# Two blocks of linear attention on one Trainium2 core: sums of x and of wq for the joint pair of q groups made in the k half and in o2 and kept, instead of being made in the joint stage

## The chip, the cores and the metric

One Trainium2 chip, one core. The time is the device time of one execution in microseconds, median of several runs. TensorE (PE) multiplies, with its weight loads shown apart (PEld); VectorE (DVE) and ScalarE (ACT) work element by element on 128 partitions; GpSimd (POOL) here does almost nothing but issue DMAs, as does SyncE (SP). DMAs move data between DRAM and the on-chip memory (SBUF); TensorE writes to PSUM.

## The reference

Two independent blocks, A and B, each with x of 2048 x 640, wqkv of 640 x 1920 and wo of 640 x 640, all fp32; 32 heads of width 20. For each block:

```python
qkv = (x @ wqkv)            # split into q, k, v, 32 heads of 20
phi = lambda t: jnp.where(t > 0, t + 1, jnp.exp(t)) + 1e-6
pq, pk = phi(q), phi(k)
kv = einsum("bhsd,bhse->bhde", pk, v)
z  = einsum("bhsd->bhd", pk)
num = einsum("bhqd,bhde->bhqe", pq, kv)
den = einsum("bhqd,bhd->bhq", pq, z)[..., None] + 1e-6
out = (num / den) @ wo      # heads put together
```

The two outputs stand side by side in one array of 2048 x 1280.

## The kernel before, in words

Every fp32 product is three products of rounded parts: a high part (`hi`, a ScalarE copy that rounds to the type fp32r) and a low part (`lo`, what is left, a VectorE subtraction in `low`, line 164). `mm3` (lines 174 to 176) adds hi x hi, lo x hi and hi x lo in PSUM.

x is handled in tiles of 128 rows, two tiles are a pair (p = 0 to 15), four tiles a group (0 to 3 of block A, 4 to 7 of block B).

**The k half.** For each pair k = x wk is made by a scheme with seven products in place of eight (`product`, `combine`): x is cut into quarter blocks A11 to A22 and a rest A5, and besides the raw parts it uses the sums S1 to S4 of them (`x_sum`, line 455). `x_parts` splits each of these into hi and lo; S1 and S3 lie in tiles `ksh`/`ksl`, which take turns between two buffers. Then comes phi (`ek`), its parts `pkh`, `pkl`, and G = x^T phi(k) gathered in `gacc` through PSUM `psg`. From G come KV, then M = KV wo, which is stored to DRAM (`md`, POOL, line 866), read back to `wst` (line 209), summed for the seven-product scheme, split into `fsh` and `fsl` (lines 902 and 164) and stored in DRAM (`fdmh`, `fdml`, POOL, line 911). Of the raw parts, the low ones are stored in DRAM too (`store_xt`, tile `xd`, SP, lines 247 to 260), and phi(k) goes out as `zd` (POOL, line 569). The order is one of jobs with a number for their place (`job`, `SHIFT`, `MOVED`), sorted by `perform`.

**The q half.** The line of stages is q0, q1, o0, q2, o1, q3, o2, q4, o3, q5, o4, r, o5, o6, o7. A q stage multiplies one group of x by wq, adds phi and builds the denominators (`acc` spread over DRAM as `da`, inverted, gathered as `rd`, line 1022); the division (line 1029), its split (`dah`, `dal`) and the sums of divided parts (`sr`, split into `dsh`, `dsl`) follow. An o stage multiplies by the forms of M and writes output rows (POOL, lines 1338 and 1340). Work beside TensorE is hung on slots of these stages with `at(slot, f)`, moved by an offset in the table `AT`.

**The joint stage r** (`qpair`, 46 slots of three 128x512 matmuls) makes q of the last two groups, 6 and 7, together, with the seven-product scheme over pairs of groups. Slots 0 and 1 use part 21; 2 to 7 part 11; 8 to 11 the sum S1 with the weight sum T; 12 to 15 S2 with `w23`; 16 to 21 part 12; 22 to 24 part 15; 25 to 31 S3 and 25; 32 to 39 part 22 with the weight sums Z and D, and 25; 40 to 45 S4. Its operands are made on the way there:

- wq of block B is loaded a second time (`load_w("w", ...)`), its sums are made in o3 and o4 (`wsum1`, `wsum2`, `wlast`), split and stored to DRAM (`wsmall`, tiles `wdT`, `wdZ`, `wdD`, line 1124), and read over the parts of wq no longer needed (`wback`, line 1140);
- the raw blocks of x are loaded (`load_xs`, line 1157), S1 to S4 are made from them in place by VectorE (`xs_sum`, line 1163), and split by ScalarE (`xs_split`, line 1179) and VectorE (line 164). The low parts of 11, 12 and 22 come from `xd` (line 1182), those of x5, the fifth chunk, from `xd` as well (line 1193), into a buffer that is shared with `sr`;
- `keep7` and `copy` (line 345) move PSUM `pa` to SBUF, so that the next product can use the bank.

Loads issue on SP in program order, and a queue's instruction waits for the buffer that it writes.

Of the kernel before, what the change touches and what calls it, by code (L numbers as in the profile page):

```python
# [15 lines left out]
DH = 20  # L16
# [90 lines left out]
def tile_linear_attn_pair(ctx: ExitStack, tc: tile.TileContext, ins, out: bass.AP):  # L107
# [22 lines left out]
    NGR = len(GROUPS)  # L130

# [106 lines left out]
    def store_xt(p, i):  # L238
        u, q = divmod(p, 2)
        lo = f32(ka[p, min(i, 1)][1])  # L240
        if u >= NU - 2:
            j = p - 2 * (NU - 2)
            if NU - 2 not in xd:
                xd[NU - 2] = dram.tile([P, NC, 2, 4, P], F32, name=f"xd{NU - 2}")
            d = xd[NU - 2][:, :, int(i == 1), j]
            if i == 0:
                nc.sync.dma_start(d[:, 0:4], lo)
# [13 lines left out]

    def load_xraw(u, c):
        b, g = divmod(u, NG)
# [193 lines left out]
    def pair_jobs(p, spots):  # L457
# [6 lines left out]
        x_parts(p, "S1", a + 1, [("s2", p)])  # L464
# [6 lines left out]
        x_parts(p, "S3", a + 1, [("s3", p)])  # L471
# [320 lines left out]

    def kv_hi(b, g):
        r = DH * GROUPS[g][1]
        t = kvt[b, g]
        kvt[b, g] = [base.tile([r, r], F32R, name=f"kv{x}", tag=f"kv{x}", bufs=6) for x in "hl"] + [t]
        nc.scalar.activation(kvt[b, g][0], t, AF.Copy)
# [283 lines left out]
    def wslots(k):  # L1081

        if k == 0:
            for c in (0, 2, 4):
                wst["w", 1, c] = stage("wst")
            wraw["x", 0], wraw["z", 0] = stage("wx"), stage("wz")
            for c in (1, 3):
                wst["w", 1, c] = stage("wst")
        else:
            wraw["x", 1], wraw["z", 1] = stage("wx"), stage("wz")  # L1090
            for a in ("11", "21", "22"):
                for c in range(2):
                    xw[a, c] = stage("xs")[:, :512]

    def wsum1(k):
        m, n = wst["w", 1, k], wst["w", 1, 2 + k]
        x = wraw["x", k]
        tt = nc.vector.tensor_tensor
        tt(x[:, HQ:2 * HQ], n[:, HQ:2 * HQ], m[:, HQ:2 * HQ], op=OP.subtract)
        tt(m[:, HQ:2 * HQ], m[:, HQ:2 * HQ], m[:, :HQ], op=OP.subtract)  # L1100

    def wsum2(k):
        m, n = wst.pop(("w", 1, k)), wst.pop(("w", 1, 2 + k))
        x, z = wraw["x", k], wraw.pop(("z", k))
        tt = nc.vector.tensor_tensor
        tt(x[:, :HQ], n[:, HQ:2 * HQ], m[:, HQ:2 * HQ], op=OP.subtract)
        tt(z[:, :HQ], n[:, :HQ], x[:, :HQ], op=OP.subtract)
        wraw["T", k] = m[:, :2 * HQ], 1
        wraw["Z", k] = z[:, :2 * HQ], 0

    def wlast(k):
        m = wst.pop(("w", 1, 4))
        nc.vector.tensor_tensor(m[:, HQ:2 * HQ], m[:, :HQ], m[:, HQ:2 * HQ], op=OP.subtract)
        wraw["D", k] = m[:, :2 * HQ], 1

    def wsmall_lo(kind, k):
        t, at = wraw[kind, k]
        h = [t[:, i * HQ:(i + 1) * HQ] for i in range(2)]
        nc.vector.tensor_tensor(h[at].bitcast(F32R), h[at], h[1 - at], op=OP.subtract)

    def wsmall_store(kind, k):
        t, at = wraw.pop((kind, k))
        d = dram.tile([P, 2 * HQ], F32, name=f"wd{kind}{k}")
        nc.gpsimd.dma_start(d, t)
        wsm[kind, k] = d, at

    def wsmall(kind, k):

        t, at = wraw[kind, k]
        h = [t[:, i * HQ:(i + 1) * HQ] for i in range(2)]  # L1130
        nc.scalar.activation(h[1 - at].bitcast(F32R), h[at], AF.Copy)
        later(1, wsmall_lo, kind, k)
        later(2, wsmall_store, kind, k)

    def wback(kind, k):
        d, at = wsm.pop((kind, k))
        i, c = {"T": (k, HQ), "Z": (0, k * HQ), "D": (1, 0)}[kind]
        for j, t in enumerate(whl["q", 1, i]):
            src = (1 - at, at)[j]
            nc.sync.dma_start(f32(t)[:, c:c + HQ], d[:, src * HQ:(src + 1) * HQ])  # L1140

    def w23_split(k):
        x = wraw.pop(("x", k))
        w23[k] = [base.tile([P, D], F32R, name=f"wf{t}", tag=f"wo{t}", bufs=2)[:, :2 * HQ] for t in "hl"]
        split(*w23[k], x[:, :2 * HQ])

    def xspan(b, c, t):
        return ins[b]["xt"][c * P:(c + 1) * P, (NG - 2) * 512:].rearrange("p (j t s) -> p t j s", t=2, s=P)[:, t]
# [10 lines left out]
    def xs_sum(n, c):  # L1159
        a11, a21, a22 = (xw.get((a, c)) for a in ("11", "21", "22"))  # L1160
        o, x, y, op = {1: (a22, a21, a22, OP.add), 2: (a22, a22, a11, OP.subtract),
                       3: (a21, a11, a21, OP.subtract), 4: (a22, xw.get(("12", c)), a22, OP.subtract)}[n]
        nc.vector.tensor_tensor(o, x, y, op=op)

    RAW = {"S1": "22", "S2": "22", "S4": "22", "S3": "21", "22": "22b"}

# [5 lines left out]
    def xs_split(a, c):  # L1172

        if a == "11":
            for k in range(2):
                xform("21", k)
        hi, lo = xform(a, c)
        src = xw[RAW.get(a, a), c]
        nc.scalar.activation(hi, src, AF.Copy)
        if a in ("11", "12", "22"):  # L1180
            k, t = chunk_of(a, c)
            nc.sync.dma_start(f32(lo).rearrange("p (j s) -> p j s", s=P), xd[NU - 2][:, k, t])
        else:
            later(1, low, lo, src, hi)
# [5 lines left out]
    def split_x5(t):  # L1190
        r = x5[t] = q2[0].tile([P, 2, 512], F32R, name="x5", tag="sr", bufs=2)
        nc.scalar.activation(r[:, 0], xw["5", t], AF.Copy)
# [115 lines left out]
    def outmm(u):  # L1308
# [14 lines left out]
        for s, (n, q) in enumerate(order):  # L1323
# [5 lines left out]
            where = [4 * g + 2 * q + t if u < NU - 2 else 4 * (NG - 2) + 2 * (2 * q + t) + (u == NU - 2) for t in range(2)]  # L1329
# [571 lines left out]
```

## Time and profile before

| | |
|---|---|
| median of 3 runs | 570.87 us (570.82 to 572.21) |
| the profiled execution | 571.82 us, of which the span of its instructions is 570.0 |
| TensorE busy | 561.5 us (98%) |
| VectorE, ScalarE, GpSimd busy | 441.1, 338.8, 87.2 us |
| moved by DMA | 131.53 MB, mean 231 GB/s |
| joint stage r | 481.04 to 515.86 us |

Rows of the timeline give the start, the length and the engine, then line, operation and tiles, and in brackets how long the engine stood idle before it and what released it. A group's row has the count after x, then busy time and mean ns. `x<-xd` means that tile x is written from tile xd. Times of DMA rows on SP and POOL are those of the issue; the landing is given separately.

### The profile page before, as it was taken

The page shows a single profiled execution, that of the slowest core. Times are in us where ns is not written, and L with a number is a line of the kernel's source. Part 1 is how long each engine was busy: PE and PEld are TensorE (multiplying, and loading weights), DVE is VectorE, ACT ScalarE, POOL GpSimd, SP SyncE. Part 2 cuts the span into 40 slices and gives each one's busy share as a digit, 9 for nine tenths or more (in the row PEclk, how much of TensorE's full clock was granted, in tenths as well). Part 3 has the DMA queues.
Part 4 walks back from the last instruction along what each step waited for, and adds up shares of the span by engine and source line. Part 5 has one row for each costly group of instructions (what it writes and reads, how often), then busy time and mean ns, then how long its engine had stood idle before and what let it go on. Part 6 is the DMA issues. An engine that isn't in the chain of part 4 may idle for free.

```text
span 570.0 us, 9167 instructions
## 1 busy us (share of the span) xinstructions
PE 561.5 (98%) x3219; PEld 508.7 (89%) x3219; DVE 441.1 (77%) x755; ACT 338.8 (59%) x635; POOL 87.2 (15%) x146
## 2 busy tenths in 40 slices
PE   9999999999999999999999999999999999999997
PEld 7989999898989988988888898898989888779997
DVE  6888798886684878878845987959668688979881
ACT  6874667672676874755737754737537274684441
POOL 0111133320011211232201103120012201000110
PEclk9999999999999999999999999999999999999999
DMA  8869789999895877989997977754568998820322
GB/s 282 234 154 260 179 243 309 268 333 353 294 246 123 202 197 156 357 207 270 356 317 228 347 229 240 248 164 159 175 214 280 308 390 248 264 81 0 131 93 92
DMA packets 85270, 131.53 MB, mean 231 GB/s; under 512 B 10088, under 2 KB 47592, under 8 KB 85224
## 3 DMA queue, kind: packets, MB, share of 16 engines
q1 hardware_dynamic: 72376, 89.75, 49.1%
q0 software_dynamic: 12560, 40.97, 26.0%
q8 instruction: 25, 0.41, 0.3%
q10 hardware_dynamic: 288, 0.23, 0.1%
q14 instruction: 21, 0.17, 0.1%
HBM read 77.09 MB, written 50.68 MB: 224 GB/s over the span
## 4 chain that ended last, share of the span: by engine, by line
PE 68%; DVE 12%; DMA 8%; issue 5%; ACT 3%; SPq 2%; POOL 0%; DVEq 0%; POOLq 0%; ACTq 0%
PE pa L341 15%; PE pe L341 7%; PE psg L176 7%; PE psg L175 7%; PE psg L174 7%; PE psk L602 5%; PE psb L341 5%; PE psq L174 4%; PE psq L176 4%; PE psq L175 4%; DMA wst<-in_B_wq 2%; PE pskv L784 2%; DMA xs<-in_B_xt 2%; DMA da<-acc 1%; DVE dsl L164 1%
## 5 line engine op out<-in xcount | busy, mean ns | idle before, releaser
L176 PE MATMUL psg<-pkh,xnl 128*128 128x512 f32 x160 | 62.8, 392 | 0.2 <-DVE xnl L164 0.2
L175 PE MATMUL psg<-pkl,xnh 128*128 128x512 f32 x160 | 62.8, 393 | 0.0
L174 PE MATMUL psg<-pkh,xnh 128*128 128x512 f32 x160 | 62.8, 392 | 0.0
L174 PE MATMUL psq<-xqh,wqh 128*128 128x512 f32 x150 | 59.1, 394 | 0.0
L176 PE MATMUL psq<-xqh,wql 128*128 128x512 f32 x150 | 58.5, 390 | 0.0
L175 PE MATMUL psq<-xql,wqh 128*128 128x512 f32 x150 | 58.4, 389 | 0.0
L345 ACT ACTIVATE o<-pa 128x320 f32<-128x320 f32 x64 | 27.6, 437 | 49.7 <-PE pa L341 49.6
L569 POOL DMA_DIRECT2D zd<-ek x30 | 26.2, 874 | 132.8 <-DVE ek L561 54.0
L345 ACT ACTIVATE ko<-pa 128x320 f32<-128x320 f32 x52 | 22.4, 432 | 36.7 <-PE pa L341 36.5
L176 PEld LDWEIGHTS psg<-pkh,xnl 128*128 128x128 f32 x160 | 30.0, 188 | 7.1 <-DVE xnl L164 0.8
L175 PEld LDWEIGHTS psg<-pkl,xnh 128*128 128x128 f32 x160 | 30.0, 188 | 5.8 <-DVE pkl L577 0.5
L174 PEld LDWEIGHTS psg<-pkh,xnh 128*128 128x128 f32 x160 | 30.1, 188 | 5.2
L176 PEld LDWEIGHTS psq<-xqh,wql 128*128 128x128 f32 x150 | 28.2, 188 | 6.0
L174 PEld LDWEIGHTS psq<-xqh,wqh 128*128 128x128 f32 x150 | 28.2, 188 | 5.7 <-ACT xqh L279 0.3
L175 PEld LDWEIGHTS psq<-xql,wqh 128*128 128x128 f32 x150 | 28.2, 188 | 5.4
L647 DVE TENSOR_TENSOR gacc<-psg,gacc 128x512 f32<-128x512 f32 (+2 forms) x42 | 25.6, 628 | 8.9 <-PE psg L176 8.9
L573 ACT ACTIVATE pkh<-ek,epst 128x640 fp32r<-128x640 f32 x32 | 25.9, 824 | 11.0 <-DVE ek L561 10.9
L1029 DVE SCALAR_TENSOR_TENSOR pq<-pq,rd 128x1280 f32<-128x1280 f32 x16 | 23.2, 1482 | 10.7 <-DMA rd<-da 10.7
L437 ACT ACTIVATE ksh<-sx 128x512 fp32r<-128x512 f32 x26 | 16.2, 629 | 25.2 <-DVE sx L455 25.0
L561 DVE SCALAR_TENSOR_TENSOR ek<-ek,ko 128x640 f32<-128x640 f32 x32 | 26.2, 820 | 6.0 <-ACT ko L558 3.4
L577 DVE SCALAR_TENSOR_TENSOR pkl<-ek,pkh 128x640 fp32r<-128x640 f32 x32 | 25.9, 820 | 5.7 <-ACT pkh L573 5.7
L967 DVE SCALAR_TENSOR_TENSOR pq<-pq,rq 128x512 f32<-128x512 f32 x30 | 20.6, 687 | 8.5 <-ACT rq L966 8.5
(290 smaller groups left out, 1781.9 us busy)
## 6 DMA issues: line engine op xcount, KB each, us to landing
zd<-ek POOLq DMA_DIRECT2D x32, 320.0 KB, 5.2
out<-o POOLq DMA_DIRECT2D x28, 320.0 KB, 4.2
xql<-xd SPq DMA_DIRECT2D x24, 256.0 KB, 4.6
xt<-in_B_xt_tiles SPq DMA_DIRECT2D x16, 320.0 KB, 4.4
xn<-in_B_x SPq DMA_DIRECT2D x16, 320.0 KB, 4.7
xqs<-in_A_xt SPq DMA_DIRECT2D x20, 256.0 KB, 6.4
fdmh<-fsh POOLq DMA_DIRECT2D x14, 320.0 KB, 4.4
fdml<-fsl POOLq DMA_DIRECT2D x14, 320.0 KB, 4.9
```

What stands on the lines that cost most here:

```text
L174: nc.tensor.matmul(o, whi, xhi, start=first, stop=False)
L175: nc.tensor.matmul(o, whi, xlo, start=False, stop=False)
L176: nc.tensor.matmul(o, wlo, xhi, start=False, stop=last)
L341: nc.tensor.matmul(o, x, y, start=start and m == r == 0, stop=m == len(terms) - 1 and r == 2, skip_group_check=True)
L345: nc.scalar.activation(x, y, AF.Copy)
L561: nc.vector.scalar_tensor_tensor(ek[n], ek[n], 1.0, rk[n], op0=OP.min, op1=OP.add)
L569: nc.gpsimd.dma_start(zacc[b], e, accum_op=OP.add)
L573: nc.scalar.activation(pk[n][0], ek[n], AF.Identity, bias=epst)
L577: nc.vector.scalar_tensor_tensor(lo, ek[n], EPS, f32(hi), op0=OP.add, op1=OP.subtract)
L602: nc.tensor.matmul(kps["c", n][h], plain_x(n, c)[i], plain_w(c)[j][:, h * HF:(h + 1) * HF], start=(c == 0 and i == j == 0), stop=(c == NC ...
L647: nc.vector.tensor_tensor(o, x, o, op=OP.add)
L1029: nc.vector.scalar_tensor_tensor(p, p, EPS, r, op0=OP.add, op1=OP.mult)
```

## The change

- **Groups are joined in another order.** `TG` maps the q groups' places: groups 5 and 6 (pairs 10 to 13) are the joint pair, and group 7 is done alone as the sixth q stage.
- **Kept forms of x.** In the k half, hi and lo of S1 and S3 of pairs 10 to 13 are stored to DRAM by POOL (`store_s`, 16 stores of 256 KB, tiles `sd`); with pairs as quarter blocks the S1 and S2 (S3 and S4) of the joint stage are two halves of what is stored. The joint stage reads them (`load_s`, 16 loads of 256 KB, on POOL and SP) and makes no sums and no splits of sums.
- **Sums of wq at its first load.** `wsum1`, `wsum2` and `wlast` run in o2 on the chunks that the first load brought. T, Z and D stay in SBUF in a tile `kept`, which takes the place of the split KV (`kvs`, now one tile); only the sum for `w23` goes to DRAM and back (two stores, two loads). The second load of wq, five stores and ten loads of 128 KB go. `wback` becomes a split of the kept sum by ScalarE and VectorE.
- **Low parts placed apart.** `xs_lo` and `x5_lo` load the low parts of 11, 12, 22 and x5 at slots of their own, not with the splits of the high parts.
- phi, mix and sums of the joint stage's halves are hung up to four slots earlier, and `AT` has other offsets.

```diff
+    TG = list(range(NG)) + [NG, NU - 1, NG + 1, NU - 2]
+    J0 = 2 * TG[NU - 2]
...
+    def store_s(p, i, k):
+        if (i, k) not in sd:
+            sd[i, k] = dram.tile([P, 2, 2, 4, P], F32, name=f"sd{i}{k}")
+        nc.gpsimd.dma_start(sd[i, k][:, :, :, p - J0], f32(ks[p, i][k]))
...
+    def s_stores(p, i, spot, what):
+        if J0 <= p < J0 + 4:
+            for k in range(2):
+                job(("ss", p, i, k), spot + k, store_s, p, i, k, after=[("xl", p, what)])
...
     def wsum1(k):
-        m, n = wst["w", 1, k], wst["w", 1, 2 + k]
-        x = wraw["x", k]
+        m, n = wst["q", 1, k], wst["q", 1, 2 + k]
+        x = wraw["x", k] = f32(base.tile([P, D], F32R, name="wx", tag="woh", bufs=2))
         tt = nc.vector.tensor_tensor
         tt(x[:, HQ:2 * HQ], n[:, HQ:2 * HQ], m[:, HQ:2 * HQ], op=OP.subtract)
-        tt(m[:, HQ:2 * HQ], m[:, HQ:2 * HQ], m[:, :HQ], op=OP.subtract)
+        tt(kept("T", k), m[:, HQ:2 * HQ], m[:, :HQ], op=OP.subtract)
...
     def wback(kind, k):
-        d, at = wsm.pop((kind, k))
         i, c = {"T": (k, HQ), "Z": (0, k * HQ), "D": (1, 0)}[kind]
-        for j, t in enumerate(whl["q", 1, i]):
-            src = (1 - at, at)[j]
-            nc.sync.dma_start(f32(t)[:, c:c + HQ], d[:, src * HQ:(src + 1) * HQ])
+        hi, lo = (t[:, c:c + HQ] for t in whl["q", 1, i])
+        split(hi, lo, kept(kind, k))
...
-    def xs_sum(n, c):
-        a11, a21, a22 = (xw.get((a, c)) for a in ("11", "21", "22"))
...
-        nc.vector.tensor_tensor(o, x, y, op=op)
...
+    def load_s(n, c):
+        i, f = divmod(n - 1, 2) if n < 3 else (1, n - 3)
+        for k, t in enumerate(xform(f"S{n}", c)):
+            (nc.sync if n == 2 or n > 2 and k else nc.gpsimd).dma_start(f32(t).rearrange("p (j s) -> p j s", s=P), sd[i, k][:, f, c])
...
+    for k in range(2):
+        i = 1 + 4 * k
+        at(("o", h - 1, i), wsum1, k)
+        at(("o", h - 1, i), wsum2, k)
+        at(("o", h - 1, i + 1), wx_store, k)
+        at(("o", O - 1, 9 + k), wx_load, k)
+        at(spot(4 + 4 * k), w23_split, k)
+    at(("o", h - 1, 11), wlast)
...
+        at(("o", O, 5 + c), load_s, 1, c)
+        at(("r", 2), load_s, 2, c)
+        at(("o", O, 7 + 3 * c), wback, "T", c)
+        at(("r", 6 + 2 * c), xs_lo, "12", c)
+        at(("r", 13 + c), load_s, 3, c)
+        at(("r", 2 + c), load_x5, c)
+        at(("r", 24 + c), load_s, 4, c)
```

TensorE's order stays, but for one product of the denominators that comes a product later. On POOL, at the end of the k half's stretch in which pairs 10 to 13 are made, there stood (line, tile written and read, shape; `md` is M, `fdmh` and `fdml` the forms of M):

```order
L866 DMA md_2178<-mev 20x4x640
L569 DMA zd_1927<-ek 128x640
L911 DMA fdmh_2854<-fsh 128x640
L911 DMA fdmh_2903<-fsh 128x640
L911 DMA fdml_2905<-fsl 128x640
```

and now:

```order
L256 DMA sd_2182<-ksl 512x1x128
L570 DMA zd_1927<-ek 128x640 x3
L873 DMA md_2171<-mev 20x4x640
L256 DMA sd_2068<-ksh 512x1x128
L256 DMA sd_2091<-ksl 512x1x128
L570 DMA zd_1927<-ek 128x640
L256 DMA sd_2172<-ksh 512x1x128
L918 DMA fdmh_2862<-fsh 128x640
L256 DMA sd_2182<-ksl 512x1x128
L918 DMA fdmh_2912<-fsh 128x640
```

Four stores of S of pair 13 came between the last M and the first forms; the other twelve stand earlier.

On VectorE, from the last reciprocal of the joint pair's predecessor to the split of its divided parts, there stood (`xs` the sums of x, line 1163; `o` output rows):

```order
L1016 RECIPROCAL da<-da 128x128
L1163 TENSOR_TENSOR xs<-xs 128x512
L348 TENSOR_TENSOR o_3690<-pe,o_3690 128x320
L1163 TENSOR_TENSOR xs<-xs 128x512 x2
L164 TENSOR_TENSOR xql<-xs,xqh 128x512
L348 TENSOR_TENSOR o_3690<-pe,o_3690 128x320
L164 TENSOR_TENSOR xql<-xs,xqh 128x512
L1163 TENSOR_TENSOR xs<-xs 128x512
L348 TENSOR_TENSOR o_3690<-pe,o_3690 128x320
L164 TENSOR_TENSOR xql<-xs,xqh 128x512
L1029 SCALAR_TENSOR_TENSOR pq<-pq,rd 128x5x256 x2
L1163 TENSOR_TENSOR xs<-xs 128x512 x2
```

and now (`kept` holds the sums of wq):

```order
L1023 RECIPROCAL da<-da 128x128
L344 TENSOR_TENSOR o_3692<-pe,o_3692 128x320
L152 TENSOR_TENSOR wql<-kept,wqh 128x256
L344 TENSOR_TENSOR o_3692<-pe,o_3692 128x320 x2
L1036 SCALAR_TENSOR_TENSOR pq<-pq,rd 128x5x256 x2
L1055 TENSOR_TENSOR sr<-pq 128x512
L1056 TENSOR_TENSOR sr<-sr,pq 128x512
L152 TENSOR_TENSOR dal<-pq,dah 128x1024
```

Between the reciprocal and the division (`pq<-pq,rd`) the sums and low parts of x are gone, and one low part of `kept` has come.

On SP, from the gather of the reciprocals into the joint stage, there stood:

```order
L1022 DMA rd<-da 32x4x128 x4
L1140 DMA wqh<-wdT_5332 128x256
L1140 DMA wql<-wdT_5332 128x256
L1140 DMA wqh<-wdT_5559 128x256
L1140 DMA wql<-wdT_5559 128x256
L1157 DMA xs<-in_B_xt 128x4x128 x2
L1188 DMA x_5763<-in_B_xt 128x4x128
```

and now:

```order
L1029 DMA rd<-da 32x4x128 x4
L1139 DMA xs<-in_B_xt 128x4x128
L1165 DMA xqh<-sd_2068 128x512
L1165 DMA xql<-sd_2091 128x512
L1169 DMA x_5691<-in_B_xt 128x4x128
L1165 DMA xqh<-sd_2068 128x512
L1165 DMA xql<-sd_2091 128x512
L1169 DMA x_5703<-in_B_xt 128x4x128
```

Four loads of S2 (256 KB each) stand where four loads of T's parts (128 KB each) stood, and x5's raw parts have come between them.

More of the change, by code (lines that the diff above doesn't have):

```diff
@@ L795, in kv_hi @@
         t = kvt[b, g]
-        kvt[b, g] = [base.tile([r, r], F32R, name=f"kv{x}", tag=f"kv{x}", bufs=6) for x in "hl"] + [t]
+        if b not in kvs_:
+            kvs_[b] = base.tile([P, 2 * NGR, 6 * DH], F32R, name="kvs", tag="kvs", bufs=1)
+        kvt[b, g] = [kvs_[b][:r, 2 * g + k, :r] for k in range(2)] + [t]
         nc.scalar.activation(kvt[b, g][0], t, AF.Copy)
@@ L1079, in tile_linear_attn_pair, with kept @@
     xw, xf, x5 = {}, {}, {}
[L1081 to L1093, printed above, removed]
+    def kept(kind, k):
+        if "kept" not in wsm:
+            wsm["kept"] = base.tile([P, 12 * 6 * DH], F32, name="kept", tag="kvs", bufs=1)
+        c = {"T": 0, "Z": 2, "D": 4}[kind] + k
+        return wsm["kept"][:, c * HQ:(c + 1) * HQ]
@@ L1116, in wsmall_lo @@
[L1116 to L1133, printed above, removed]
+        tt(x[:, :HQ], n[:, HQ:2 * HQ], kept("T", k), op=OP.subtract)
```

132 lines of the change are left out of this document (54 added, 78 removed).

## The prediction

> **What bounds the kernel now.** I read the page first, then the span cut into stretches, then the waits of TensorE, and last the rows around each stall of the stage that the change rewrites. In the page, busy time, share and instructions of each engine:
>
> ```profile
> span 570.0 us, 9167 instructions
> PE 561.5 (98%) x3219; PEld 508.7 (89%) x3219; DVE 441.1 (77%) x755; ACT 338.8 (59%) x635; POOL 87.2 (15%) x146
> ```
>
> TensorE (PE) is busy for 561.5 of 570.0 us and the change leaves its work as it is (one short product moves by a place), so nothing but the 8.5 us of idle TensorE time can be won, less what lies before the first and behind the last matmul. Cut into stretches (length, then busy time of PE, PEld, DVE, ACT, POOL, then clock, DMA share, GB/s):
>
> ```profile
> 399.00:456.00 57.00, 56.38 (x320) 51.23 (x320) 41.51 (x68) 27.27 (x54) 9.70 (x18) 1.00 0.74 244
> 464.76:481.04 16.28, 16.11 (x109) 15.85 (x108) 14.00 (x26) 7.05 (x17) 1.62 (x3) 1.00 0.88 277
> 481.04:515.86 34.82, 32.79 (x140) 25.60 (x139) 31.07 (x46) 25.25 (x45) 1.62 (x3) 1.00 0.54 171
> 515.86:568.00 52.14, 49.81 (x327) 47.78 (x325) 37.73 (x53) 20.83 (x39) 4.32 (x8) 1.00 0.23 83
> 447.56:464.76 17.20, 17.20 (x78) 14.01 (x76) 14.62 (x23) 10.23 (x19) 2.96 (x6) 1.00 0.99 351
> 490.00:500.00 10.00, 8.20 (x35) 6.15 (x35) 9.96 (x14) 8.33 (x14) 0.00 (x0) 1.00 0.94 290
> ```
>
> The joint stage is 481.04 to 515.86: 46 slots of three 128x512 matmuls, 138 in all. The stretch 447.56 to 464.76, q of group 5 (75 such matmuls and no idle time), gives the undisturbed pace, 17.20 / 75 = 0.229 us; 138 of them are 31.6 us. Against 34.82 us the stage loses **3.2 us**, more than its 2.0 us of recorded idle time, because the first matmul behind a stall also steps more slowly: the row at 491.39 below starts its next after 0.34 us.
>
> The three places, in TensorE's timeline:
>
> ```profile
> 482.60 0.50 PE L175 MATMUL ps<-xql,wqh 128*128 128x512 f32 x1 [0.23 <-DVE xql L164]
> ...
> 489.55 0.39 PE L1247 MATMUL pe<-xql,wqh 128*128 128x512 f32 x1
> 489.78 0.39 PE L1247 MATMUL pe<-xqh,wql 128*128 128x512 f32 x1
> 491.39 0.50 PE L1247 MATMUL pa<-xqh,wfh 128*128 128x512 f32 x1 [1.23 <-ACT pq L345]
> 491.73 0.39 PE L1247 MATMUL pa<-xql,wfh 128*128 128x512 f32 x1
> ...
> 499.42 0.50 PE L1247 MATMUL psb<-x,wqh 128*128 128x512 f32 x1 [0.58 <-DMA x<-xd]
> ```
>
> From 489.78 to 491.39 is 1.61 us where 0.23 is the pace: 1.38 lost. Its cause stands in ScalarE's and VectorE's timelines:
>
> ```profile
> 488.67 1.24 ACT L1179 ACTIVATE xqh<-xs 128x512 fp32r<-128x512 f32 x2 [5.50 <-DVE xs L1163]
> 489.81 1.04 ACT L167 ACTIVATE dah<-pq 128x1024 fp32r<-128x1024 f32 x1
> 490.76 0.58 ACT L345 ACTIVATE pq<-pa 128x512 f32<-128x512 f32 x1
> ```
>
> ```profile
> 485.07 2.88 DVE L1029 SCALAR_TENSOR_TENSOR pq<-pq,rd 128x1280 f32<-128x1280 f32 x2
> 487.87 1.29 DVE L1163 TENSOR_TENSOR xs<-xs 128x512 f32<-128x512 f32 x2
> ...
> 494.55 1.22 DVE L164 TENSOR_TENSOR dsl<-sr,dsh 128x1024 fp32r<-128x1024 f32 x1
> ```
>
> The copy that frees pa for S2 stands on ScalarE behind the split of S2, which waits 5.50 us for a sum (L1163) that VectorE does only after the division of group 5. The third stall is a load into the buffer that `dsl` gives back:
>
> ```profile
> 495.80 0.32 SPq L1193 DMA_DIRECT2D x<-xd  x1
> ```
>
> It goes out 0.03 us after that operation's end (494.55 + 1.22 = 495.77), and TensorE begins 3.62 us later. So VectorE's lateness, 9.96 of 10 us in the stretch from 490 above, sets two of the three stalls, and the first is also a low part that it makes.
>
> **The change: the joint stage.** Durations of what goes, in the window from 464 to 516:
>
> ```profile
> L1163 DVE TENSOR_TENSOR xs<-xs 128x512 f32<-128x512 f32 x8 | 5.4, 686 | 1.9 <-DMA xs<-in_B_xt 1.9
> L164 DVE TENSOR_TENSOR xql<-xs,xqh 128x512 fp32r<-128x512 f32 x10 | 6.7, 686 | 2.2 <-ACT xqh L1179 2.1
> L1179 ACT ACTIVATE xqh<-xs 128x512 fp32r<-128x512 f32 x16 | 9.5, 625 | 11.0 <-DVE xs L1163 5.5 <-DMA xs<-in_B_xt 5.5
> L1100 DVE TENSOR_TENSOR wst<-wst 128x256 f32<-128x256 f32 x1 | 0.4, 424 | 0.0
> ```
>
> VectorE loses 8 sums and 8 low parts, 16 x 0.686 = 11.0 us, and gains five low parts of weight sums of 128x256, 5 x 0.42 = 2.1. ScalarE loses 8 high parts, 8 x 0.625 = 5.0, and gains five of 128x256, about 2 us by half the width. Of these 8.9 and 3 us none lies on the path of itself; what counts is that the division no longer has three sums and three low parts between the last products of group 4 and itself, that no sum and no split stand ahead of the copy of pa, and that `dsl` comes free sooner. From 481.25 to 485.07 VectorE did three of either (4.1 us). Without the three sums and one low part the division can begin about 2.7 us earlier, at 482.4, unless the reciprocals' load holds it; I take 483. The copy of pa then needs only pa's products (489.2 at the latest) and the `dah` of 1.04 us, which starts with the division's end near 486: free by 488, before slot 12. `dsl` ends near 491.3, and the load that goes out then lands about 495, ahead of slot 22, which at the pace falls at 481.04 + 66 x 0.229 = 496.2. All 3.2 us could go.
>
> What comes in: S2's four parts (256 KB each) are loaded on SP once slots 0 and 1 give their buffers back, 482.4 to 483.1 here, four issues and a load of x5's raw part between them. Like transfers, from issue to landing:
>
> ```profile
> xql<-xd SPq DMA_DIRECT2D x24, 256.0 KB, 4.6
> ```
>
> Five issues at 0.45 us end near 485; 485 + 4.6 = 489.6 against slots 12 (489.3) and 13 (490.0): between no wait and 1.5 us, if the queue is as full as the 0.94 of the stretch at 490. I take 0.3, nearer the lower end, since ten loads of weights (128 KB) left this stretch of SP. Two copies of pa in the second half now stand behind three more phi steps on ScalarE, which come four slots earlier; 0 to 0.5 us, taken 0.2. So **-2.7 us** (0 to -3.2).
>
> **o4 and the tail.** 464.76 to 481.04 is 0.17 us short of all busy: -0.1. Group 7's phi, mix and denominators end some ten slots x 0.69 us earlier or so, which lets the last outputs find their halves ready; the stretch from 515.86 has 52.14 - 49.81 = 2.3 us of idle time, 1.3 of it after the last matmul. Of the 1.0 left I take -0.3 (0 to -0.8).
>
> **The first load of wq, in o2.** There VectorE gains nine operations of 128x256, 9 x 0.42 = 3.8 us, in place of those in o3 and o4; the stretch from 399 has 57.00 - 41.51 = 15.5 us free on VectorE and 0.6 us of idle TensorE time. The nine also hold chunks of wq's stage longer, which moves two raw loads of x behind them: 0 to +1, taken +0.3. Ten loads, five stores and a second load of wq (1.6 MB) go; TensorE did not wait for them, so nothing is won there.
>
> **The k half.** Sixteen stores of 256 KB on POOL, about 160 to 232 us, each of 512 runs of 512 bytes. Nothing like it is on POOL now; the bounds of the issue are these rows (count, total, mean ns):
>
> ```profile
> L569 POOL DMA_DIRECT2D zd<-ek x30 | 26.2, 874 | 132.8 <-DVE ek L561 54.0 <-DVE sx L455 17.6 <-DVE gacc L647 10.8
> L1124 POOL DMA_DIRECT2D wdT<-wst x2 | 1.1, 540 | 15.2 <-DMA xs<-in_B_xt 15.2
> L247 SPq DMA_DIRECT2D xd<-kal x4: 370/374/592, 189.8 to 260.0; - x4
> ```
>
> On SP a store with the same 512 runs issues in 0.37 us, no slower than others; on POOL 128 rows cost 0.54, so at four times the rows at most 4 x 0.54 = 2.2 us. I take 0.9, the dearest POOL row, since SP's price does not follow the runs: 16 x 0.9 = 14 us of a queue that is idle here (POOL columns below).
>
> ```profile
> 160.00:195.00 35.00, 35.00 (x218) 32.21 (x217) 25.00 (x53) 24.74 (x52) 5.19 (x7) 1.00 0.77 183
> 195.00:225.00 30.00, 30.00 (x169) 27.02 (x167) 23.58 (x40) 19.66 (x35) 5.62 (x7) 1.00 0.72 165
> 225.00:245.00 20.00, 20.00 (x134) 19.48 (x133) 17.56 (x32) 13.86 (x24) 4.72 (x8) 1.00 1.03 330
> 245.00:265.00 20.00, 19.70 (x104) 17.09 (x103) 16.34 (x29) 11.04 (x19) 7.81 (x13) 1.00 0.83 234
> ```
>
> The bytes matter more: 16 x 256 KB = 4.2 MB. At 330 GB/s (a share of 1.03) they fill 12.7 us of all engines, at 165 / 0.72 = 229 GB/s 18.3; free in 160 to 225 are 35 x 0.23 + 30 x 0.28 = 16.5 us. They just fit, and the last four come at about 222 to 232, where the share is already 1.03. Behind them the first fdm stores and their reload stand, and the one chain with a row:
>
> ```profile
> 247.51 0.74 ACT L902 ACTIVATE fsh<-wst 128x640 fp32r<-128x640 f32 x1 [1.75 <-DMA fdmh<-fsh]
> 248.28 0.83 DVE L164 TENSOR_TENSOR fsl<-wst,fsh 128x640 fp32r<-128x640 f32 x1 [3.44 <-ACT fsh L902]
> ```
>
> A later landing of fdmh moves both. VectorE has 20.00 - 16.34 = 3.7 us free in 245 to 265 and has waited 3.44 of them just there, so it has little to catch up with: what slips comes partly to TensorE, which already lost 0.3 in that stretch. One MB, the last four stores, is 3.2 us of slip at 330 GB/s; I take a fifth of it, **+0.7** (0 to +4), since TensorE lost so little with the engines full.
>
> [...]
>
> **Sum:** joint stage -2.7, o4 -0.1, tail -0.3, o2 +0.3, k half +0.7: -2.1 us. The profiled execution took 571.82 us (570.0 of span and 1.8 around it), 0.95 above the median of 570.87. -2.1 from the median gives **568.8 us**, and 569.7 for an execution as slow as the profiled one.
>
> **Rivals.**
> - *The k half takes it back: slower.* The place is the queue to DRAM at 222 to 245, the mechanism the one above. It decides from a slip of some 5 us of fdmh (its landing at 247.5 moves to 252 or later), since VectorE can absorb no more than its 3.7 us; sixteen stores at 2.2 us on POOL, or at 229 GB/s, are enough: 18.3 of engine time against 16.5 free, and the last four wait behind. Then +4 to +7 and the winnings of 3.1: 571.8 to 575, middle 573.5. For it speak the share of 1.03 and the 3.44 us wait; against it that TensorE lost just 0.3 us with the share at 1.03 for 20 us. [...]
> - *S2's loads come late: no change.* SP waits for buffers of the first slots; what it queues behind is four landings of 4.6 us at a share near 1. Each of the two first slots of S2 waits 1 us, x5 and the later parts shift as well, 2 us of the 2.7 are lost again, and it ends at 570.5. For it speaks 489.6 against 489.3; against it the 0.54 share over the stage.
> - *The stores cost nothing.* TensorE is 35.00 of 35.00 and 30.00 of 30.00 busy in 160 to 225, and keeps that. All of the joint stage is won: 570.87 - 3.2 - 0.4 + 0.2 = 567.5.
>
> **How the numbers follow.** A measurement of this kernel can tell 0.3%, 1.7 us, from no change: faster is under 569.2, slower above 572.6. The sum of the forecast has 0.36 (567.6 to 570.2, 0.22 of it faster, 0.14 same); stores at nothing 0.20, all faster; S2 late 0.13, same; k half 0.31, 0.28 of it slower and 0.03 same. That is faster 0.42, same 0.30, slower 0.28. The predicted time is the forecast's, 568.8. Below, the range ends at 567.0, which leaves out only the far end of the third rival; above at 573.8, just past the middle of the k half's case, so that about 0.15 of the chance lies above it and 0.05 below.
>
> **What would show it.** Right: no sums from L1163 and no wait for the copy of pa or x<-xd in the joint stage, its length near 32 us; the division's start at 483 or before; POOL's stores of S at 0.5 to 1 us each and TensorE full until 245. Wrong: TensorE waiting on psg or psk between 160 and 270 for a low part that is late; stores of S above 2 us; S2's products waiting for a load near 489. A longer o2 would say that VectorE's nine sums are not covered.

## The result, and the profile after

The changed kernel takes 571.34 us in the median of 20 runs (570.06 to 574.37), the kernel before 571.62 in 20 runs on the same chips (568.00 to 574.21): a ratio of 1.0001, 95% interval 0.9985 to 1.0016. No difference. I had forecast 568.8. In one execution of each kernel, the joint stage is 1.7 us shorter where I had 2.7, the other stages of the q half won 3.0 us where I had 0.1, and the k half and the start took most of it back.

The page of the changed kernel:

```profile
span 568.8 us, 9177 instructions
PE 560.7 (99%) x3219; PEld 511.1 (90%) x3219; DVE 432.4 (76%) x739; ACT 335.4 (59%) x627; POOL 102.5 (18%) x167
```

VectorE has 8.7 us less to do, GpSimd 15.3 more. To see where time is won and lost I paired the matmuls of both traces, whose order is the same, and subtracted their starts, both counted from the first one. (A positive number: the changed kernel is behind.) The difference (after less before, us) at some of them:

| matmul near (us, before) | difference | what lies between |
|---|---|---|
| 200 | +0.6 | the start of the kernel |
| 214 | +4.5 | **k half: +4.0** |
| 270 | +3.5 | -0.9 at 263, where the kernel before had a short stall |
| 406 | +3.4 | nothing |
| 420 | +3.1 | o2: -0.3 |
| 450 | +2.1 | o3: -1.0 |
| 480 | +1.6 | o4: -0.4 |
| 491 | -0.5 | joint stage, to S2: -2.2 |
| 500 | 0.0 | joint stage, behind S2: +0.5 |
| 560 | -1.2 | tail: -1.2 |

One trace of each kernel stands behind this table, and single executions differ: the trace of e2 below, whose q half is the kernel before's, falls from 3.8 us behind at 406 to 3.5 at 420, 2.6 at 450 and 2.1 at 480 as well. So the table does not show that the gains of o2, o3 and o4 come from the change.

The stretches of the changed kernel around the loss (length, busy time of PE, PEld, DVE, ACT and POOL, clock, DMA share, GB/s), and the joint stage, which took 34.82 us:

```profile
195.00:200.00 5.00, 5.00 (x37) 5.00 (x35) 3.54 (x7) 3.46 (x7) 4.05 (x7) 1.00 0.78 162
200.00:205.00 5.00, 5.00 (x35) 4.91 (x34) 3.44 (x6) 2.58 (x5) 1.97 (x3) 1.00 1.02 324
205.00:210.00 5.00, 3.65 (x20) 2.87 (x18) 3.11 (x5) 2.17 (x5) 0.91 (x1) 1.00 1.04 375
210.00:215.00 5.00, 3.94 (x16) 3.94 (x17) 2.81 (x5) 3.46 (x6) 0.67 (x1) 0.66 0.73 195
...
482.68:515.85 33.17, 32.45 (x140) 25.66 (x139) 23.83 (x33) 21.67 (x39) 2.96 (x6) 1.00 0.63 212
```

In 205 to 215 TensorE is idle for 2.4 us, and then the granted clock is 0.66. The chain of it stands in rows of the timelines of POOL, SP, ScalarE and TensorE:

```profile
195.95 0.89 POOL L572 DMA_DIRECT2D zd<-ek  x1 [4.40 <-DVE sx L451]
...
197.18 1.83 POOL L256 DMA_DIRECT2D sd<-ksh  x2
198.49 2.00 POOL L256 DMA_DIRECT2D sd<-ksl  x2
...
198.63 0.33 SPq L410 DMA_DIRECT2D xn<-in_B_x  x1
...
207.83 0.74 ACT L484 ACTIVATE xnh<-xn 128x640 fp32r<-128x640 f32 x1 [2.79 <-DMA xn<-in_B_x]
...
211.06 0.63 PE L337 MATMUL pa<-wfh,kah 128*128 128x320 f32 x1 [2.41 <-ACT ko L341]
211.49 0.47 PE L337 MATMUL pa<-wfl,kah 128*128 128x320 f32 x1
```

Six stores of S (1.5 MB) issue without a pause from 197.2 to about 202, behind a store of phi(k) for which POOL had waited until 195.95 and one of M. A load of x, `xn`, issues amid them at 198.63 and is there only at 207.8, 9.2 us later, with a DMA share of 1.02 to 1.04 in 200 to 210. Before, the same load went out at 198.08 and its split began 6.4 us later, almost without a wait (0.03 us):

```profile
198.08 0.33 SPq L414 DMA_DIRECT2D xn<-in_B_x  x1
...
204.51 0.74 ACT L481 ACTIVATE xnh<-xn 128x640 fp32r<-128x640 f32 x1
```

The load had next to no time to spare. In the changed kernel ScalarE's split of it waits 2.79 us, the copy `ko<-pa` stands behind the split, and TensorE waits 2.41 us for that copy. Then its matmuls of 128x320 step by 0.27 us in place of 0.15, till 214.4.

The waits of TensorE in the changed kernel show that the joint stage's old ones are gone or smaller:

```profile
PE pa L337 <- ACT ko L341: 2.4, 1, 2.4
PE psi L1349 <- PEq L1870: 0.8, 1, 0.8
PE pe L337 <- DVE o L344: 0.5, 1, 0.5
PE psb L1230 <- DMA x<-xd: 0.4, 1, 0.4
PE pa L337 <- ACT o L341: 0.2, 1, 0.2
PE pa L1230 <- DMA xql<-sd: 0.2, 1, 0.2
```

The wait for the copy `pq<-pa` (1.2) is not there any more; x5 makes TensorE wait 0.4 where it was 0.6. S2's loads, one of the rivals, show as a wait of 0.2, but the steps of the matmuls around it lose more: the 13 steps from 490.63 to 494.51 take 3.88 us, where the pace of 0.229 us makes 2.98, so 0.9 is lost.

### The profile page after: what moved, and what is told of

It reads as the page before. It is cut to its first block, busy times and chain, and to the rows that moved or that the text cites. A ratio compares the mean times of both kernels' runs of the same rounds, so it can differ in the third digit from the quotient of the medians.

```text
span 568.8 us, 9177 instructions
## 1 busy us (share of the span) xinstructions
PE 560.7 (99%) x3219; PEld 511.1 (90%) x3219; DVE 432.4 (76%) x739; ACT 335.4 (59%) x627; POOL 102.5 (18%) x167
## 4 chain that ended last, share of the span: by engine, by line
PE 91%; DMA 3%; DVE 2%; ACT 2%; issue 1%; SPq 0%; DVEq 0%; ACTq 0%
PE pa L337 20%; PE pe L337 10%; PE psg L163 8%; PE psg L164 8%; PE psg L162 8%; PE psb L337 7%; PE psq L162 6%; PE psq L164 6%; PE psq L163 6%; PE psk L605 5%; DMA xn<-in_B_x 2%; PE pskv L787 2%; PE pa L1230 1%; DMA x<-xd 1%; DMA x<-in_B_xt 1%; PE pe L1230 1%
## 5 line engine op out<-in xcount | busy, mean ns | idle before, releaser
L155 ACT ACTIVATE dah<-pq 128x1024 fp32r<-128x1024 f32 (+2 forms) x24 | 17.7, 773 | 22.6 <-DVE pq L1036 22.6
```

## The experiments

Medians and ratios are against the kernel before, run beside each.

| run | median, us | ratio, 95% interval |
|---|---|---|
| e1: no stores of S | 566.83 | 0.9918 (0.9889 to 0.9948) |
| e2: before, with the stores | 573.82 | 1.0044 (1.0021 to 1.0068) |
| e3: four stores moved | 568.85 | 0.9956 (0.9936 to 0.9977) |
| e4: stores on SP | 572.35 | 1.0013 (0.9990 to 1.0036) |
| e5: eight stores moved | 571.23 | 1.0013 (0.9992 to 1.0034) |
| e6: before, fewer sums | 570.25 | 0.9990 (0.9973 to 1.0007) |
| e7: e5, phi steps late | 574.07 | 1.0066 (1.0039 to 1.0093) |
| e8: before, stores placed as in e5 | 574.05 | 1.0055 (1.0034 to 1.0075) |
| e9: a third placing | 569.91 | 0.9984 (0.9970 to 0.9997) |
| e10: high parts only | 568.88 | 0.9976 (0.9960 to 0.9992) |
| e11: VectorE work put back | 573.92 | 1.0060 (1.0038 to 1.0081) |
| e12: the same, placed later | 567.43 | 0.9933 (0.9909 to 0.9958) |

### The price of the stores: e1 and e2

```diff
-        if J0 <= p < J0 + 4:
+        if False:
             for k in range(2):
                 job(("ss", p, i, k), spot + k, store_s, p, i, k, after=[("xl", p, what)])
...
-            (...).dma_start(f32(t).rearrange("p (j s) -> p j s", s=P), sd[i, k][:, f, c])
+            (...).dma_start(f32(t).rearrange("p (j s) -> p j s", s=P), xd[NU - 2][:, c + 2 * f, 0])
```

> The changed kernel without its 16 stores of S in the k half; the joint stage loads the same number of bytes from the stored low parts of x instead, so the values of the last two groups are not the reference's. Theory 1 (the k half's 4.0 us, which TensorE loses between 207 and 215, come from the six stores that issue together at 197 to 200 and hold back a load of x): TensorE does not wait there, the clock stays full, and the time is 567.4 us (571.3 less 4.0, +-0.8). Rival (the loss at 207 is chance of one execution and the medians are level because the joint stage gives nothing): 571.3, within 0.3%.

Measured 566.83, 4.5 us below the changed kernel. TensorE's longest wait in the k half is now 0.3:

```profile
PE pa L337 <- ACT ko L341: 0.3, 1, 0.3
```

So all of the change but its stores is worth 0.82% (0.5 to 1.1) against the kernel before, and the stores take the same back. The rival, that the loss at 207 was chance, falls.

e2 puts `store_s` and `s_stores` into the kernel before, with the same places:

```diff
-        x_parts(p, "S3", a + 1, [("s3", p)])
+        a = x_parts(p, "S3", a + 1, [("s3", p)])
+        s_stores(p, 1, a + 2, "S3")
```

> The kernel before with the same 16 stores added at the same places of the k half, read by nobody; all else as before. Theory 1: about 4 us slower than before, 575.5 us, with a wait of TensorE near 207 for a copy on ScalarE that stands behind a late x load. Rival (volume costs nothing, or the loss needs the other changes): 571.6.

Measured 573.82, 2.5 us (1.2 to 3.9) above the kernel before; fewer than the 4 expected. In its profiled execution TensorE waits mainly at two places for the same copy, 1.16 and 1.59 us, and neither is followed by a lower clock (0.999 in the mean of the execution):

```profile
209.50 0.41 PE L348 MATMUL pa<-wfh,kah 128*128 128x320 f32 x1 [1.16 <-ACT ko L352]
238.22 0.41 PE L348 MATMUL pa<-wfh,kah 128*128 128x320 f32 x1 [1.59 <-ACT ko L352]
```

The stores alone are enough for a loss. It is smaller than in the changed kernel, without the half clock, and has a second place; why was not tried.

### Where the stores stand, or how many: e3, e5, e8, e9, e10

e3 moves the four stores of pair 12 out of the burst, behind the stores of phi(k) at 207 and 214:

```diff
+                late = {(12, 0, 0): 9.5, (12, 0, 1): 8.6, (12, 1, 0): 6.8, (12, 1, 1): 5.9}.get((p, i, k), 0)
-                job(("ss", p, i, k), spot + k, store_s, p, i, k, after=[("xl", p, what)])
+                job(("ss", p, i, k), spot + k + late, store_s, p, i, k, after=[("xl", p, what)])
```

> The changed kernel with four of the six stores that issue together at 197 to 200 moved behind the stores of phi(k) at 207 and 214; nothing else. Theory 1 (the burst): most of the 4.0 us come back, 567.5 to 568.5 us, faster than both kernels. Rival 2 (the volume of 4.2 MB on DMA engines that are nearly full is what counts, wherever it stands): the wait only moves, 571 us or so.

Measured 568.85, **faster than both kernels**, though 0.35 above the end of what was expected. Its largest wait in TensorE's list:

```profile
PE pa L337 <- ACT ko L341: 1.4, 2, 1.0
```

1.0 is left near 207, behind which two of the stores still stand ahead of the load of x; 0.4 is new at 236.7, again behind a load of `xn`. The clock stays full (1.0 in the mean of the execution). e5 moves those two and the next ones too:

```diff
+                late = {(11, 1, 0): 9.75, (11, 1, 1): 8.85, (12, 0, 0): 13.81, (12, 0, 1): 12.91, (12, 1, 0): 9.51, (12, 1, 1): 8.61, (13, 1, 0): 8.69, (13, 1, 1): 7.79}.get((p, i, k), 0)
```

> As the run with four stores moved, and further: the two stores of pair 11's S3 also behind the store of phi(k) at 207, the four of pair 12 behind those at 214 and 219, and the last two of pair 13 behind the first forms of M. Theory 1 (what costs is stores that stand ahead of a load of x which ScalarE is about to need): the waits near 207 and 235 go, 567 to 568 us, 0.8 to 1.4 below the run with four moved. Rival 2 (volume): no better than it, 568.9.

Measured 571.23: the wait near 207 is gone, as theory 1 said, and others came, so the time is that of the changed kernel. Against e1's trace it loses 2.0 us at 235, 1.4 at 265 and 1.1 at S2, whose loads make TensorE wait 0.31 and 0.85. Its stretches and the row of the first wait:

```profile
205.00:210.00 5.00, 5.00 (x30) 4.59 (x29) 3.79 (x6) 4.20 (x7) 2.44 (x3) 1.00 0.73 145
235.00:240.00 5.00, 3.75 (x26) 3.48 (x25) 4.43 (x7) 3.53 (x6) 1.08 (x2) 1.00 1.03 401
```

```profile
236.58 0.41 PE L337 MATMUL pa<-wfh,kah 128*128 128x320 f32 x1 [1.25 <-ACT ko L341]
```

The chain of this wait begins at M's store `md`. In e5 two stores of S issue ahead of it on POOL, at 217.03 and 218.04:

```profile
218.67 0.82 POOL L874 DMA_DIRECT2D md<-mev  x1
...
224.02 1.86 SPq L197 DMA_DIRECT2D wst<-md  x3
...
228.66 0.85 SPq L410 DMA_DIRECT2D xn<-in_B_x  x1
...
235.47 0.74 ACT L485 ACTIVATE xnh<-xn 128x640 fp32r<-128x640 f32 x1 [1.52 <-DMA xn<-in_B_x]
```

and in e1, where TensorE is at the same place within 0.1 us:

```profile
218.19 0.65 POOL L873 DMA_DIRECT2D md<-mev  x1 [0.72 <-ACT mev L341]
...
222.03 1.29 SPq L197 DMA_DIRECT2D wst<-md  x3
...
226.14 0.47 SPq L410 DMA_DIRECT2D xn<-in_B_x  x1
```

`md` lands 5.2 us after its issue in e5 and 3.7 in e1. SP reads M back (`wst`) right behind that landing, 5.35 and 3.84 us after `md`'s issue, and the load of x that stands behind it in SP's order goes out 2.5 us later in e5. Its own landing, 6.8 us after the issue, is near those of e1 there (4.4 to 6.6). So theory 1 is right on the wait at 207 and too narrow: in slices of 5 us the DMA share of e5 is 0.73 to 1.05 from 195 to 260, and a store that is put off can also delay a store that SP waits for, and with it every load behind. The kernel before with the stores at the places of e5 says the same:

> The kernel before with the 16 stores added, at the spread places. Theory 1: most of the 2.7 us that the stores cost at the first places go, 571.2 to 572.2 us. Rival 2 (volume): 573.8 as there.

The edit is e5's line in e2. Measured 574.05, no better than e2. The waits of that execution stand at 234 and 238 (0.77 and 1.77 us), and the clock falls behind the second (0.89 in 235 to 240, 0.77 in 240 to 245). e9 keeps four stores behind 207 and two behind 214:

```diff
+                late = {(11, 1, 0): 9.75, (11, 1, 1): 8.85, (12, 0, 0): 9.71, (12, 0, 1): 8.81, (12, 1, 0): 6.8, (12, 1, 1): 5.9, (13, 1, 0): 8.69, (13, 1, 1): 7.79}.get((p, i, k), 0)
```

> The changed kernel with the two stores of pair 11's S3 and the two of pair 12's S1 behind the store of phi(k) at 207, the two of pair 12's S3 behind that at 214, the last two of pair 13 behind the first forms of M. A mixture of the two theories (a store costs where it stands ahead of a load that is about to be needed, and all of 4.2 MB have to go somewhere between 170 and 260): no wait at 207, a small one at 235, 567.5 to 569.5 us. If volume alone counts: 570 to 571.

Measured 569.91, above the forecast of the mixture by 0.4: no wait at 207, 0.42 and 0.95 at 233 and 237. The kernel before took 570.29 beside it and 571.15 beside e1; on the latter the ratio of 0.9984 makes 570.2, which lies in the forecast of volume. The waits are those of the mixture; the time doesn't tell the two apart. e10 writes the eight high parts alone:

```diff
-            for k in range(2):
+            for k in range(1):
                 job(("ss", p, i, k), spot + k, store_s, p, i, k, after=[("xl", p, what)])
...
-            (...).dma_start(f32(t).rearrange("p (j s) -> p j s", s=P), sd[i, k][:, f, c])
+            (...).dma_start(f32(t).rearrange("p (j s) -> p j s", s=P), xd[NU - 2][:, c + 2 * f, 0] if k else sd[i, k][:, f, c])
```

> The changed kernel with only the eight stores of high parts, at their places; the low parts of S are read from the low parts of x, so the values of the joint pair are not the reference's. Without stores it was 566.8 us, with all sixteen 571.3. Volume in proportion: 569.0. Burst with a threshold (three stores, not six, stand ahead of the load at 198): under 568, with a wait at 207 under 0.5 us.

Measured 568.88, near volume in proportion (569.0), with two waits left:

```profile
210.00 0.41 PE L337 MATMUL pa<-wfh,kah 128*128 128x320 f32 x1 [1.18 <-ACT ko L341]
237.11 0.42 PE L337 MATMUL pa<-wfh,kah 128*128 128x320 f32 x1 [0.40 <-ACT ko L341]
```

No threshold: a wait of 1.18 stands where under 0.5 was expected. Half the bytes cost 0.45 of the price by the medians of e1, e10 and the changed kernel, and 0.7 by their ratios, which allow for the kernel before being 0.9 us faster beside e10 than beside e1; the intervals do not tell these apart.

### Who issues them: e4

```diff
-        nc.gpsimd.dma_start(sd[i, k][:, :, :, p - J0], f32(ks[p, i][k]))
+        nc.sync.dma_start(sd[i, k][:, :, :, p - J0], f32(ks[p, i][k]))
```

> The changed kernel with the 16 stores issued by SP in place of POOL. Theory 1: the bytes are the same, SP's order puts loads between some of the stores and others behind them, so the loss near 207 changes in size but does not go: 569 to 573 us. Rival 3 (POOL's way of issuing is what costs, by its queue or by its descriptors): the loss goes, 567.5 us.

Measured 572.35. The wait near 207 is 2.7 us, but it comes about in another way:

```profile
202.97 0.87 SPq L410 DMA_DIRECT2D xn<-in_B_x  x1
...
207.66 0.74 ACT L484 ACTIVATE xnh<-xn 128x640 fp32r<-128x640 f32 x1 [3.07 <-DMA xn<-in_B_x]
```

On SP the load of `xn` stands behind four of the stores. It goes out 4.3 us later than in the changed kernel and lands 4.7 us after that, where it took 9.2. The loss doesn't go, as theory 1 said, but since it has moved from the landing to the issue, the run doesn't decide whether POOL's way of issuing has a part in the changed kernel's loss. In this run the rival of S2's loads shows as well, and the clock falls at both places:

```profile
PE pa L337 <- ACT ko L341: 2.7, 1, 2.7
PE pa L1230 <- DMA xql<-sd: 0.9, 1, 0.9
PE psi L1349 <- PEq L1870: 0.8, 1, 0.8
PE pa L1230 <- DMA xqh<-sd: 0.7, 1, 0.7
```

and in its stretches:

```profile
205.00:215.00 10.00, 7.32 (x36) 6.62 (x35) 6.30 (x10) 5.67 (x9) 1.76 (x2) 0.83 1.06 266
490.00:500.00 10.00, 8.45 (x29) 6.16 (x28) 7.09 (x11) 8.30 (x16) 1.10 (x2) 0.83 1.00 324
```

### The joint stage and the tail: e6, e7, e11, e12

e6 takes two of the four sums from the kernel before, which is four operations:

```diff
-        nc.vector.tensor_tensor(o, x, y, op=op)
+        if n in (1, 4):
+            nc.vector.tensor_tensor(o, x, y, op=op)
```

> The kernel before without the sums of x for S2 and S3 (four of 0.69 us on VectorE), so that the splits read raw blocks and the values of the joint pair are not the reference's. Theory 4 (VectorE's lateness ahead of and behind the division sets the waits of the joint stage): the wait for the copy of pa (1.2) goes and the one for x5's low part shrinks, 1.5 to 2.4 us less: 568.7 to 569.6. Rival 5 (the copy of pa is held by the split of divided parts or by loads as well): the wait only moves, 570.6 or more.

Measured 570.25, between the two theories and not told from no change. In its trace the wait for x5 is gone, and the copy of pa still makes TensorE wait 0.9 where it was 1.2; the joint stage takes 33.07 us in place of 34.82, a gain in the range of theory 4, but TensorE waits 1.36 in o3 where it was 0.59. The medians leave it open. To ask the other way I put VectorE's work back into e1, as repeats of one low part:

```diff
+    def again():
+        hi, lo = (t[:, 0 + HQ:HQ + HQ] for t in whl["q", 1, 1])
+        for _ in range(14):
+            low(lo, kept("T", 1), hi)
+
+    at(("o", O, 12), again)
```

> The kernel without stores in the k half, with 14 low parts of 128x256 (5.9 us of VectorE, made again from the same numbers) put back ahead of the division of group 5. VectorE waited about 4 us there. Theory 4 (VectorE's lateness set the waits of the joint stage): the division begins 2 to 3 us later, the copy of pa comes 1.5 to 2.5 us after it is needed, TensorE waits that long: 568.3 to 569.5 us. Rival 5 (the gain came from taking the splits of S2 from ahead of that copy on ScalarE, or from earlier loads): 566.8 to 567.5.

Measured 573.92, 7 us more than e1 for 5.9 us of work, far past what was expected. TensorE waits 5.87 us for the copy of pa, and the clock is at half for 6.8 us from within that wait (0.994 in the mean of the execution); but ScalarE's row shows that I had added a second cause:

```profile
487.86 1.06 ACT L155 ACTIVATE dah<-pq 128x1024 fp32r<-128x1024 f32 x1 [10.18 <-DVE pq L1036]
492.50 0.60 ACT L341 ACTIVATE pq<-pa 128x512 f32<-128x512 f32 x1 [3.58 <-DMA out<-o]
```

The copy writes into memory that an output row of group 4 leaves free, and that row's last sum stood behind my work. e12 therefore places ten of the repeats behind that sum, at the head of the division:

```diff
     def divide(u, h):
+        if u == NU - 3 and h == 0:
+            again()
```

> As the run with VectorE's work put back, but ten of the low parts (4.5 us) and behind the last output sum of group 4, directly ahead of the division, so that no output row and no buffer waits for them. Theory 4: the division begins 2.2 us later than without them (483.5 against 481.3), the split and the copy of pa behind it follow, and TensorE waits about 2 us for that copy: 568.8 us, or 570.5 if the clock falls to half for 3.4 us behind the wait. Rival 5 (the division had that much room): 566.8 to 567.3.

Measured 567.43, 0.6 above e1 by the medians (the intervals overlap). The rows of VectorE without and with the work, and TensorE's row with it:

```profile
478.52 0.49 DVE L344 TENSOR_TENSOR o<-pe,o 128x320 f32<-128x320 f32 x1 [0.82 <-PE pe L337]
481.34 1.49 DVE L1036 SCALAR_TENSOR_TENSOR pq<-pq,rd 128x1280 f32<-128x1280 f32 x1 [2.32 <-DMA rd<-da]
```

```profile
479.72 4.56 DVE L152 TENSOR_TENSOR wql<-kept,wqh 128x256 fp32r<-128x256 f32 x10
484.19 2.88 DVE L1038 SCALAR_TENSOR_TENSOR pq<-pq,rd 128x1280 f32<-128x1280 f32 x2
...
488.70 0.50 PE L1232 MATMUL pa<-xqh,wfh 128*128 128x512 f32 x1 [1.26 <-ACT pq L341]
```

With TensorE 0.8 us later at 480 in this execution, the division is 2.1 us later, of which TensorE loses 1.1 at S2: the copy had about 0.7 us of room in e1 (ready at 485.24 + 0.58 = 485.82, needed at 486.50). VectorE's lateness ahead of the division does set that wait, but it is only part of the old one. It also shows that the division itself now waits for its reciprocals, 2.32 us here.

e7 is e5 with the phi steps, mixes and sums of the joint stage at their old slots:

```diff
-    for u, c, i in ((NU - 1, 0, 24), (NU - 1, 1, 25), (NU - 1, 4, 26), (NU - 2, 2, 29), (NU - 2, 3, 32), (NU - 2, 0, 35),
-                    (NU - 2, 1, 38), (NU - 2, 4, 40), (NU - 1, 2, 44), (NU - 1, 3, 46)):
+    for u, c, i in ((NU - 1, 0, 28), (NU - 1, 1, 29), (NU - 1, 4, 31), (NU - 2, 2, 32), (NU - 2, 3, 35), (NU - 2, 0, 36),
+                    (NU - 2, 1, 38), (NU - 2, 4, 40), (NU - 1, 2, 47), (NU - 1, 3, 48)):
```

> The run with all stores spread, but the phi steps of the joint stage, their mixes and sums at the slots of the kernel before (two to four slots later). Theory 6 (the tail's gain of 1.2 us and the division of the last groups come from the earlier phi steps): 0.7 to 1.2 us slower than that run, in the stretch behind the joint stage. Rival 7 (the tail gains because the whole joint stage is less crowded on VectorE and ScalarE): no difference over 0.3 us.

Measured 574.07, 2.8 above e5, more than twice what theory 6 expected. Paired with e5's trace it loses 3.0 us behind the joint stage, at two places:

```profile
519.70 0.41 PE L337 MATMUL pe<-fh,dsh 128*128 128x320 f32 x1 [0.72 <-DVE pq L344]
532.68 0.41 PE L337 MATMUL pe<-fh,dsh 128*128 128x320 f32 x1 [1.67 <-DVE o L344]
```

So the earlier phi steps are a part of the change that it can't do without. This is no price of the step in the kernel before, where the rest of `AT` is another.

## Why the prediction was wrong

**The k half: the term that failed.** I took +0.7 for the stores, with 0 to +4 as its bounds. They cost 4.5 us by the medians of the changed kernel and e1, and 4.7 by the ratios, with some 2 us either way: far from 0.7, and not told from the upper bound. The two traces put 3.6 of it at 207 to 214 and 0.5 at S2. The amount was in the working: 16.5 us of room against 12.7 to 18.3 us of added engine time, "they just fit". The step that failed is the next one: I let only the last four stores slip, and placed their harm on `fdmh` at 242 to 250. The room is not to be had evenly. Twelve stores stood in the part that I had counted as fitting, six of them issued within 5 us, and a load that fell among them took 9.2 us. I looked for the late landing where a wait was already seen, and not at every load that is issued into a burst. The right reading was that this load of x is wanted 6.4 us after its issue (198.08 to 204.51 before), so that a landing of 9.2 us is 2.8 us of waiting for ScalarE and 2.4 for TensorE.

**The clock.** No term stood for it. The 2.41 us without work were followed by 3.4 us of half clock, 1.7 more lost.

**The rival that the k half takes it back** had the right mechanism, full engines and a late landing (a DMA share of 1.02 to 1.04, 9.2 us), at a wrong place, with a fair price (+4 to +7). It ended as no change and not as slower, because the winnings were larger than the 3.1 I had set against it.

**POOL.** The stores issue in 1.07 to 1.12 us each in the mean, rows below, where I took 0.9 with 2.2 as the upper end. The load that is late in the changed kernel is one of SP's and doesn't wait for POOL's queue.

```profile
L256 POOL DMA_DIRECT2D sd<-ksl x8 | 8.3, 1124 | 0.0
L256 POOL DMA_DIRECT2D sd<-ksh x8 | 8.1, 1066 | 1.3 <-ACT ksh L433 1.3
```

Of the 0.31 that the rival of the k half had, 0.05 stood for issues dearer than those 2.2 us. No run shows one: the longest of the 16 issues took 1.59 us, and those of the burst followed each other every 0.63 to 0.67 us, with VectorE busy for 3.54 of 5.00 us in the stretch at 195.

**The joint stage** had the right mechanism and too large a gain: -2.7 forecast, -1.65 in the changed kernel (34.82 to 33.17 us) and -2.15 in e1 (478.32 to 510.99, 32.67 us). All three waits went or shrank. What was missed against the pace is 0.9 at S2's loads, where I took 0.3, and 0.7 at x5's low part, which I took to land in time. Its step on the division was wrong: I had it begin at 483, and it begins at 486.2, which is 484.6 on the clock of the kernel before, half a microsecond earlier than the 485.07 there. It waits 2.82 us for `rd`. The copy of pa became free all the same, since only `dah` stands ahead of it now.

**S2's loads** cost 0.9 in the changed kernel, of which 0.2 is recorded as a wait; that rival had put 2 us on them. In e5 their waits are 1.16 us together, and 1.55 with the stores on SP, so it was near.

**o2 and o3.** I took +0.3 for o2, and nothing for the loads and sums that leave o3. The paired traces give -0.3 and -1.0, and e2's trace, without the change of these stages, gives much the same. In o3 of the kernel before TensorE waits 0.59 us at 446 for a sum that stands on VectorE behind the spread denominators (`da<-acc`); in the changed kernel's traces the wait is gone. In e1 VectorE has the last sum of the denominators done 1.6 us earlier there, counted from TensorE's place (434.54 against 437.50, of which TensorE's lead is 1.3). Whether that comes from the load of wq that is gone, from another order of VectorE's work or from the execution was not tried.

**The tail** gave 1.2 in place of 0.3. From the joint stage's end to the end of the span it is 53.5 to 54.2 us in the four traces with the tail of the kernel before (before, e2, e6, e8) and 52.7 to 53.2 in the nine with the new one, so some of the 1.2 is the execution's. e7 shows what the earlier phi steps carry.

**The sum.** Winnings of 4.7 us (e1's ratio of 0.9918 on 571) where I had 2.8, and a k half of 4.5 where I had 0.7.

## What to carry to other kernels

Free DMA time in a stretch is not room for a transfer (here 16.5 us of it, and a load among six stores took 9.2): look at each load that is wanted soon after its issue, take the time between the two (6.4 us for that one), and ask what will be queued beside it. Do the same for each store whose landing SP waits for, since the loads that stand behind it slip too, by 2.5 us in e5. Stores that stood in order behind a late store came out together here, six of them within 5 us. A new placing is tested by the next sensitive load, not by the one that was mended: e3, with four stores moved, beats both kernels at 568.85 us, and e5, with eight moved, is back at 571.

## What the runs showed of the hardware

**Waits of 1.77 to 5.87 us, and two of under 0.9 close together, were followed by half clock; single ones of up to 1.67 were not.** Behind the 2.41 us of the changed kernel the clock was at half for 3.4 us. So it was, by the shares, behind the 2.68 of e4 (0.83 in 205 to 215) and the 1.77 of e8 (0.89 and 0.77 in 235 to 245), and behind the two waits of 0.68 and 0.87 us in e4, which end 1.4 us apart (0.83 in 490 to 500). With the 5.87 of e11 came 6.8 us of it. Waits of 1.67 in e7, 1.59 in e2 and 1.23 in the kernel before were followed by none. In the changed kernel's record of the clock the stretch at half lasts 3.413 us, and those at full speed ahead of it and behind it 204.80 and 354.99 us, 60 and 104 times as long. The length of the waits alone does not divide the two groups, since e4's two make 1.55 us together; what does was not tried.

**Stores of 512 runs of 512 bytes issued on POOL in 1.07 to 1.12 us in the mean, those of 128 rows in 0.88.** So it was in the changed kernel, with the 16 stores of S and the 30 of phi(k). Outside the bursts those of S took 0.75 to 0.89; before, those of phi(k) took 0.87.
